# Seven half-block products per chunk pair in the first layer of the second MLP

## The chip, the cores and the metric

The kernel runs on one core of one Trainium2 chip. The metric is the device time of one execution in microseconds (us); less is better. TensorE (PE in the profile) multiplies matrices, VectorE (DVE) and ScalarE (ACT) do elementwise work, GpSimd (POOL) issues a few DMAs here, and SyncE (SP) issues nearly all of them.

## The reference

Attention (a pooled and a banded local softmax attention, added) makes `x` of 2304 tokens x 512. Two MLPs follow, one after the other, each with d_model 512 and d_ff 2048 and its own weights (the host passes them as float64 words):

```python
x = _moe_ref(x)    # h = x @ w_in;  g = h * cos(h);        x = g @ w_out
return _moe2_ref(x)  # h = x @ w_in;  g = maximum(h, 0)**2;  return g @ w_out
```

## The kernel before

Everything is kept transposed: the model or hidden dimension lies on the 128 partitions, the tokens along the free dimension. An fp32 value is split into a high and a low float32r part (`split`: ACT copies to the high part, DVE subtracts to get the low one), and one fp32 product is three matmuls: high weight by high data, high by low, low by high (`mm3`, L641 to L644).

The program has two phases, one for each MLP. A phase goes through five rounds of tokens (`ROUNDS`: four of 512, one of 256), and a round through 16 chunks `f` of 128 hidden units. For each chunk, `mlp_h` (L646) makes 4 x 3 matmuls into a `ps` bank, ACT and DVE apply the nonlinearity and split the result to `gh`, `gl`, and `mlp_o` (L715), some chunks later, makes 4 x 3 matmuls into the four `acc` banks, which sum over all 16 chunks. After the last chunk each `acc` is copied to an `e` tile (two buffers) and stored, to `x2d` in DRAM after phase 0, to the output after phase 1. The first MLP's phase is interleaved with attention units (`unit_g`, `unit_l`); attention for batches 1 to 3 loads pooled sums through accumulating DMAs on the POOL queue.

Weights: `convert` (L253) loads 512 KB of float64 words into a `raw` tile, makes float32 of them with three integer operations on DVE (L265, L272, L277) and splits them. The first-layer weights of the phase stay in 16 `w1` tiles; phase 1's replace phase 0's chunk by chunk during the last round of phase 0 (L838). The second-layer weights are converted in the first round of a phase, saved to `w2d`, and loaded again (`w2`, 512 KB a chunk, three buffers) in every later round.

The order of the program on every engine is written out by `Plan` (L48): each operation has an engine, an assumed cost, a due time (`key`) and what it reads and writes; a list scheduler puts on each engine, in simulated time, what can start first, among equals the one due first. A table `OFF` of offsets shifts due times by operation name and stage. What comes out is a fixed order for each engine; on the chip every instruction waits for its own semaphores, and those queued behind it on its engine wait with it.

Of the kernel before, what the change touches and what calls it, by code (L numbers as in the profile page):

```python
# [40 lines left out]
ORDER = [[0, 1, 2, 3, 4], [0, 2, 3, 4, 1]]  # L41
# [6 lines left out]
class Plan:  # L48
    """The order of the program: operations are put on their engines when what they need is there."""
# [3 lines left out]
    IN_TURN = ("rawi", "rawo", "w2", "p", "pt", "q", "v", "t")  # L53
# [30 lines left out]
    def slow(used, warm, t, cost):  # L84
        """The tensor engine runs at half its clock in a window that follows a mostly idle one."""
# [13 lines left out]
    def order(self):  # L99
# [23 lines left out]
        def room(inst):  # L123
            tag = inst[0]
            held = got[tag]
            if tag in self.IN_TURN and turn[tag][len(held)] != inst:
                return None
            if len(held) < self.bufs[tag]:
                return 0.0
            last = [end[i] for i in self.users[held[-self.bufs[tag]]]]  # L130
            return None if None in last else max(last) + 0.1

        while len(out) < n:
            best = None
            for e, c in cand.items():
                t_min, pick = None, []
                for i in c:
                    t = max(free[e], ready_at[i])
                    for inst in ops[i][5]:
                        x = room(inst)  # L140
# [16 lines left out]
            for inst in new:  # L157
                got[inst[0]].append(inst)
            begin[i] = t
# [42 lines left out]
def body(ctx: ExitStack, tc: tile.TileContext, qb, kw, vw, qp, kp, vp, wi, wo, masks, ident, out_t):  # L202
# [4 lines left out]
        "mx": 4, "sm": 4, "gh": 3, "gl": 3, "e": 2, "acc": 1, "ps": 4,  # L207
    }

    const = ctx.enter_context(tc.tile_pool(name="const", bufs=1))  # L210
    pool = ctx.enter_context(tc.tile_pool(name="work", bufs=2))
    psum = ctx.enter_context(tc.tile_pool(name="psum", bufs=1, space=PSUM))

# [3 lines left out]
    kz = [const.tile([128, 2, 2, PR, KT], F32, name=f"kz{i}") for i in range(2)]  # L217
    pz = [const.tile([128, PR, 2, 2, QT], F32, name=f"pz{i}") for i in range(2)]
# [3 lines left out]
    w1 = [const.tile([128, 2, KD, 128], F32R, name=f"w1_{f}") for f in range(NF)]  # L222
    xh = const.tile([128, KD, 512], F32R, name="xh")
    xl = const.tile([128, KD, 512], F32R, name="xl")
    xr = const.tile([128, KD, XR], F32, name="xr")
    qn_sb = const.tile([128, PR, SD], F32, name="qn_sb")
    qd_sb = const.tile([128, PR, 3, 2, 48], F32, name="qd_sb")
    kd_sb = const.tile([128, PR, SD], F32, name="kd_sb")
    vd_sb = const.tile([SD // 2, 2, DM], F32, name="vd_sb")
    up_sb = const.tile([128, PR, S], F32, name="up_sb")  # L230
    x2d = nc.dram_tensor("x2_dram", [128, KD, NT], F32, kind="Internal").ap()
    w2d = [nc.dram_tensor(f"w2_dram_{p}", [NF, 128, 2, DM], F32, kind="Internal").ap() for p in range(2)]
# [5 lines left out]
    def new(inst, shape, dtype=F32, space=None):  # L238
        p = psum if space else pool
# [14 lines left out]
    def convert(key, lead, name, src, hi, lo, wh, wl):  # L254
        raw, m, a = ("raw" + name[0],) + name[1:], ("wm", name), ("wa", name)

        def load():
            new(raw, [128, 512, 2], I32)
            if wh[1]:
# [21 lines left out]
        op("SP", 1.46, key - lead, load, w=[raw] + wh[0], new=[raw] + wh[1])  # L281
# [3 lines left out]
        split(key + 0.03, 512, hi, lo, lambda: T[a].bitcast(F32), [a], (wh[0], []), wl)  # L285

    def conv_wi(key, lead, ph, f):
        convert(
            key, lead, ("i", ph, f), wi[ph, f],
            lambda: w1[f][:, 0].rearrange("p k n -> p (k n)"), lambda: w1[f][:, 1].rearrange("p k n -> p (k n)"),  # L290
            ([("w1h", f)], []), ([("w1l", f)], []),
        )

    def get_w2(key, ph, r, f):
        w2 = ("w2", ph, r, f)
        if r == ORDER[ph][0]:
# [334 lines left out]

    def load_x2(r, key):
        t0, n = ROUNDS[r]
        for o, c, m in ring(t0, n):
            op(
                "SP", m / 175, key, lambda o=o, c=c, m=m: nc.sync.dma_start(
                    out=xr[:, :, c:c + m], in_=x2d[:, :, t0 + o:t0 + o + m]),
                r=[("x2d", r, c2) for c2 in range(KD)], w=xtok(t0 + o, m),
            )
# [6 lines left out]
    def mlp_h(ph, r, f, key):  # L646
# [3 lines left out]
        for k in range(KD):  # L650
            def f_h(k=k):
                if k == 0:
                    new(hp, [128, 512], space=PSUM)
                mm3(
                    T[hp][:, 0:n], w1[f][:, 0, k], w1[f][:, 1, k], xh[:, k, 0:n], xl[:, k, 0:n], k == 0, k == KD - 1
# [3 lines left out]
                "PE", 3 * (n / 2400 + 0.0025), key + 0.01 * k, f_h,  # L659
                r=[("w1h", f), ("w1l", f), ("xh", k), ("xl", k)], w=[hp], new=[hp] if k == 0 else [],  # L660
# [6 lines left out]
        if ph == 0:  # L667
            def f_k():
                new(ki, [128, 512], I32)
                nc.scalar.activation(out=tt(ki), in_=tt(hp), func=AF.Copy, scale=1.0 / TWO_PI)  # L670

            def f_r():
                new(t, [128, 512])
                nc.vector.scalar_tensor_tensor(  # L674
                    out=tt(t), in0=tt(ki), scalar=-TWO_PI, in1=tt(hp), op0=OP.mult, op1=OP.add
                )

            def f_sin():
                nc.scalar.activation(out=tt(t), in_=tt(t), func=AF.Sin, scale=-1.0, bias=halfpi[:, 0:1])  # L679

            def f_g():
                nc.vector.tensor_tensor(out=tt(t), in0=tt(t), in1=tt(hp), op=OP.mult)  # L682
# [240 lines left out]
```

## Time and profile before

| | us |
|---|---|
| median of 3 runs | 955.86 |
| the 3 runs | 956.81, 955.05, 955.86 |
| span of the profiled execution | 956.2 |
| PE / DVE / ACT busy in the span | 927.4 / 519.2 / 471.7 |

The span runs from the first to the last instruction of one profiled execution; no other time of that execution is shown, so its own time is taken as its span, which lies 0.3 us above the median. Matmuls are pipelined, so that the profile gives each a duration longer than the distance to the next; a rate is read from the distance between starts.

### The profile page before, as it was taken

The numbers are of one execution on the slowest core, as the hardware profiler recorded it, in microseconds if no ns is written. First come the engines' busy times: TensorE is split into PE (matmuls) and PEld (weight loads), VectorE is DVE, ScalarE is ACT, GpSimd is POOL, SyncE is SP. The second block draws the span as 40 slices with busy tenths as digits, with TensorE's granted clock in tenths as the row PEclk, the third lists the DMA queues.
The fourth block names the chain that finished last, engine by engine and source line by source line (L and its number), as shares of the span: only waits on it lengthen the run. The fifth ranks groups of instructions, "written<-read, shape, count | busy, mean of one in ns | idle before, by whom it ended". The sixth has DMA issues, their size and how long they took to land.

```text
span 956.2 us, 13754 instructions
## 1 busy us (share of the span) xinstructions
PE 927.4 (97%) x5312; PEld 765.8 (80%) x5312; DVE 519.2 (54%) x953; ACT 471.7 (49%) x962; POOL 36.8 (4%) x53
## 2 busy tenths in 40 slices
PE   7889999989999999999999999999999999999997
PEld 7677787889877778787888888888888888888897
DVE  7878999645744457344787786662223223222322
ACT  3757787757747767455655533341223223222322
POOL 3030000300210000000000000000000000000000
PEclk9999999989999999999999999999999999999999
DMA  9996665975972242322765675554235233423364
GB/s 283 290 271 173 220 215 207 261 220 175 263 178 89 78 146 96 121 97 90 268 214 177 220 245 196 176 202 140 89 109 165 88 96 107 150 90 109 115 216 133
DMA packets 59857, 162.06 MB, mean 169 GB/s; under 512 B 6544, under 2 KB 16528, under 8 KB 59792
## 3 DMA queue, kind: packets, MB, share of 16 engines
q1 hardware_dynamic: 55184, 149.38, 47.2%
q0 software_dynamic: 4608, 11.80, 6.3%
q8 instruction: 42, 0.69, 0.3%
q14 instruction: 23, 0.19, 0.1%
HBM read 134.94 MB, written 26.21 MB: 169 GB/s over the span
## 4 chain that ended last, share of the span: by engine, by line
PE 85%; DMA 10%; DVE 2%; ACT 1%; SPq 1%; issue 0%; POOL 0%; ACTq 0%; DVEq 0%; POOLq 0%
PE acc L642 14%; PE acc L643 13%; PE acc L644 13%; PE ps L642 13%; PE ps L643 13%; PE ps L644 13%; DMA kd_sb<-in_kp_dram 2%; DMA rawi<-in_wi_dram 2%; PE ps L583 2%; PE ps L546 2%; DMA w<-w_dram 1%; DMA mask_f<-in_masks_dram 1%; PE ps L471 1%; DMA v<-in_vw_dram 1%; DMA qn_sb<-in_qp_dram 1%; PE ps L505 1%
## 5 line engine op out<-in xcount | busy, mean ns | idle before, releaser
L642 PE MATMUL acc<-gh,w 128*128 128x512 f32 (+1 forms) x640 | 240.6, 376 | 4.8 <-DMA w<-w_dram 3.7
L642 PE MATMUL ps<-xh,w 128*128 128x512 f32 (+1 forms) x640 | 241.3, 377 | 2.0 <-DVE t L682 2.0
L644 PE MATMUL ps<-xh,w 128*128 128x512 f32 (+1 forms) x640 | 238.6, 373 | 0.0
L643 PE MATMUL ps<-xl,w 128*128 128x512 f32 (+1 forms) x640 | 238.4, 373 | 0.0
L643 PE MATMUL acc<-gl,w 128*128 128x512 f32 (+1 forms) x640 | 238.1, 372 | 0.0
L644 PE MATMUL acc<-gh,w 128*128 128x512 f32 (+1 forms) x640 | 237.4, 371 | 0.0
L693 ACT ACTIVATE t<-ps 128x512 f32<-128x512 f32 (+1 forms) x80 | 44.5, 556 | 235.8 <-PE ps L644 235.8
L696 DVE SCALAR_TENSOR_TENSOR t<-ps,t 128x512 f32<-128x512 f32 (+1 forms) x80 | 50.9, 638 | 200.5 <-ACT t L693 200.5
L642 PEld LDWEIGHTS acc<-gh,w 128*128 128x128 f32 x640 | 120.9, 189 | 29.6 <-issue 4.8
L642 PEld LDWEIGHTS ps<-xh,w 128*128 128x128 f32 x640 | 120.8, 189 | 26.6 <-DVE t L682 2.9
L643 PEld LDWEIGHTS acc<-gl,w 128*128 128x128 f32 x640 | 121.1, 189 | 22.5 <-DVE gl L248 0.2
L644 PEld LDWEIGHTS acc<-gh,w 128*128 128x128 f32 x640 | 120.8, 189 | 22.3
L644 PEld LDWEIGHTS ps<-xh,w 128*128 128x128 f32 x640 | 120.5, 188 | 22.1
L643 PEld LDWEIGHTS ps<-xl,w 128*128 128x128 f32 x640 | 120.6, 188 | 20.7
L248 DVE TENSOR_TENSOR gl<-t,gh 128x512 fp32r<-128x512 f32 (+1 forms) x160 | 101.6, 636 | 64.5 <-ACT gh L245 61.1
L245 ACT ACTIVATE gh<-t 128x512 fp32r<-128x512 f32 (+1 forms) x160 | 93.6, 586 | 77.3 <-DVE t L696 41.9
L682 DVE TENSOR_TENSOR t<-t,ps 128x512 f32<-128x512 f32 (+1 forms) x80 | 50.3, 632 | 53.1 <-ACT t L679 52.7
L670 ACT ACTIVATE ki<-ps 128x512 int32<-128x512 f32 (+1 forms) x80 | 43.7, 549 | 64.6 <-PE ps L644 63.8
L674 DVE SCALAR_TENSOR_TENSOR t<-ki,ps 128x512 f32<-128x512 int32 (+1 forms) x80 | 50.4, 631 | 32.9 <-ACT ki L670 32.0
L687 ACT ACTIVATE t<-t 128x512 f32<-128x512 f32 (+1 forms) x80 | 46.8, 584 | 26.4 <-DVE t L674 25.5
L679 ACT ACTIVATE t<-t,halfpi 128x512 f32<-128x512 f32 (+1 forms) x80 | 54.1, 679 | 1.8
L245 ACT ACTIVATE w<-wa 128x512 fp32r<-128x512 f32 x64 | 39.8, 624 | 10.1 <-DVE wa L277 9.8
(66 smaller groups left out, 755.7 us busy)
## 6 DMA issues: line engine op xcount, KB each, us to landing
w<-w_dram SPq DMA_DIRECT2D x128, 512.0 KB, 3.3
rawo<-in_wo_dram SPq DMA_DIRECT2D x32, 512.0 KB, 4.3
rawi<-in_wi_dram SPq DMA_DIRECT2D x32, 512.0 KB, 4.9
w_dram<-w SPq DMA_DIRECT2D x32, 512.0 KB, 3.0
v<-in_vw_dram SPq DMA_DIRECT2D x20, 256.0 KB, 4.8
kz<-in_kw_dram SPq DMA_DIRECT2D x40, 128.0 KB, 4.9
q<-in_qb_dram SPq DMA_DIRECT2D x20, 232.0 KB, 4.8
vd_sb<-in_vp_dram POOLq DMA_DIRECT2D x16, 288.0 KB, 7.1
```

The source lines that it names most:

```text
L245: nc.scalar.activation(out=hi(), in_=src(), func=AF.Copy)
L248: nc.vector.tensor_tensor(out=lo(), in0=src(), in1=hi().bitcast(F32), op=OP.subtract)
L642: nc.tensor.matmul(ps, w_hi, r_hi, start=first, stop=False)
L643: nc.tensor.matmul(ps, w_hi, r_lo, start=False, stop=False)
L644: nc.tensor.matmul(ps, w_lo, r_hi, start=False, stop=last)
L670: nc.scalar.activation(out=tt(ki), in_=tt(hp), func=AF.Copy, scale=1.0 / TWO_PI)
L674: nc.vector.scalar_tensor_tensor(out=tt(t), in0=tt(ki), scalar=-TWO_PI, in1=tt(hp), op0=OP.mult, op1=OP.add)
L679: nc.scalar.activation(out=tt(t), in_=tt(t), func=AF.Sin, scale=-1.0, bias=halfpi[:, 0:1])
L682: nc.vector.tensor_tensor(out=tt(t), in0=tt(t), in1=tt(hp), op=OP.mult)
L687: "ACT", act(n), key + 0.2, lambda: nc.scalar.activation(out=tt(t), in_=tt(t), func=AF.Abs), w=[t]
L693: nc.scalar.activation(out=tt(t), in_=tt(hp), func=AF.Relu)
L696: nc.vector.scalar_tensor_tensor(out=tt(t), in0=tt(hp), scalar=0.0, in1=tt(t), op0=OP.max, op1=OP.mult)
```

## The change

Phase 1 becomes a form of its own; phase 0 keeps its rounds and its code, while the cost that the plan assumes for one matmul of n columns goes from n/2400 + 0.0025 to n x 0.0004375 + 0.007.

- Phase 1 has three rounds R of 768 tokens, each in two halves of 384, and goes through 8 pairs `p` of chunks. The first layer of a pair (2 chunks, 2 x 256 inner, 2 halves of tokens) is done as seven products in place of eight. Each product takes 6 matmuls of 384 columns (`big_h`) into one of two PSUM banks `pp0`, `pp1`, in turn. ACT copies the first product out; DVE adds the others from PSUM into `ua` and `c` tiles (seven additions of 384 columns).
- The data operands (`operands`, once per round) are seven split tiles made from `xr`: 4 subtractions and 7 splits of 768 columns.
- The weight operands (`conv1`, once per pair, emitted at the third round of phase 0) are made from the raw words, with 4 sums of 256 columns and splits of 2 x 256, 2 x 256, 2 x 256 and 256 columns, and stored to a DRAM tensor `w1d` (seven blocks of 256 KB a pair). `big_h` loads each block for each product again, into the `gh` and `gl` buffers (three each), once the last `gh` and `gl` of phase 0 are written. The conversion of the second MLP's `w_in` in the last round of phase 0 goes.
- The square of the relu, and its split, are done at 768 columns (`big_g`: DVE, ACT, DVE). The parts lie in the memory of `xh`, `xl` and one `w1` tile.
- The second layer (`big_o`) makes, for each chunk and each of 4 output blocks, three matmuls of 512 and three of 256 columns; the 256-column results of two blocks share a bank (`acx0`, `acx1`). After a round there are four `e` tiles for the 512 part and two for the shared banks, through the same two buffers.
- The attention tiles sit in a pool of their own, which is closed and reused for the operands.

```diff
+            for h in range(2):
+                def f_p(h=h, ws=ws, x=x, b=b):
+                    ww = [T[ws][:, i, 128 * h:128 * h + 128] for i in range(2)]
+                    xx = [T[xo(R, x)][:, i, h] for i in range(2)]
+                    mm3(T[f"pp{b}"][:, 0:HALF], ww[0], ww[1], xx[0], xx[1], h == 0, h == 1)
...
+            if nm == "p1":
+                op(
+                    "ACT", act(HALF), k, lambda ps=ps: nc.scalar.activation(out=uv(0), in_=ps(), func=AF.Copy),
+                    r=[pp], w=[u],
+                )
+            elif nm == "p2":
+                add(k, lambda: part(0, 0), lambda: uv(0), [u], [c[0]])
+            elif nm == "p6":
+                add(k, lambda: uv(0), lambda: uv(0), [], [u])
+            elif nm == "p7":
+                add(k, lambda: uv(1), lambda: uv(0), [u], [v])
+            elif nm == "p5":
+                add(k, lambda: part(1, 1), lambda: uv(1), [v], [c[1]])
+                add(k + 0.01, lambda: uv(0), lambda: uv(0), [], [u])
+            elif nm == "p3":
+                add(k, lambda: part(0, 1), lambda: uv(0), [u], [c[0]])
+                big_g(R, p, 0, k + 0.02)
+            else:
+                add(k, lambda: part(1, 0), lambda: uv(1), [v], [c[1]], sub=True)
+                big_g(R, p, 1, k + 0.02)
...
+            op("SP", 0.73, k - 12.0, f_w, r=[("w1d", p, n // 2), ("last",)], w=[ws], new=[ws])
...
+            op("PE", 3 * 0.231, k, f_b, r=g, w=[("accb", c)])
+            op("PE", 3 * 0.119, k + 0.01, f_x, r=g, w=[("acx", c // 2)])
...
+            op("SP", 1.46, k - 12.0, load, r=[("conv",)], w=[raw], new=[raw])
+            op("DVE", dve2(512), k, f1, r=[raw], w=[m], new=[m])
+            op("DVE", dve(512), k + 0.01, f2, r=[raw, m], w=[a], new=[a])
+            op("DVE", dve(512), k + 0.02, f3, r=[raw], w=[a])
...
+            op("ACT", act(256 * n), k, f_hi, r=[t], w=[st], new=[st])
+            op("DVE", dve(256 * n), k + 0.01, f_lo, r=[t], w=[st])
+            op("SP", 0.73 * n, k + 0.5, f_st, r=[st], w=[("w1d", p, j)])
...
+    for R in range(NBIG):
+        if R:
+            operands(R, big_when[R - 1, 1], big_when[R - 1, 2], big_step * 5)
+        for p in range(PAIRS):
+            t_p = big_when[R, p]
+            for i in range(2):
+                get_w2b(t_p + big_step * (0.8 + 0.5 * i), R, 2 * p + i)
+            q = (R, p - 1) if p else (R - 1, PAIRS - 1)
+            for i in range(2):
+                if i:
+                    big_h(R, p, t_p, big_step)
+                if R or p:
+                    big_o(q[0], 2 * q[1] + i, big_when[q] + big_step * (LAG + 0.5 * i), big_step / 2)
```

## Rows read from the trace of the kernel before

**Rows 1.** The page: busy time, share of the span and instructions of each engine.

```profile
PE 927.4 (97%) x5312; PEld 765.8 (80%) x5312; DVE 519.2 (54%) x953; ACT 471.7 (49%) x962; POOL 36.8 (4%) x53
```

**Rows 2.** Stretches: length, busy time of each engine, granted clock, DMA share, GB/s.

```profile
160.00:200.00 40.00, 35.17 (x253) 31.15 (x252) 24.31 (x58) 27.89 (x59) 9.75 (x13) 0.95 1.00 282
240.00:280.00 40.00, 39.02 (x265) 32.02 (x264) 24.05 (x46) 23.52 (x42) 10.18 (x13) 1.00 0.97 239
...
480.00:520.00 40.00, 40.00 (x174) 32.28 (x173) 32.34 (x54) 21.82 (x37) 0.00 (x0) 1.00 0.57 194
...
680.00:720.00 40.00, 40.00 (x174) 32.31 (x173) 11.67 (x17) 10.92 (x19) 0.00 (x0) 1.00 0.29 93
```

**Rows 3.** Timeline of PE in phase 1: 100 starts of 512 columns, 176 of 256.

```profile
699.49 0.40 PE L644 MATMUL ps<-xh,w 128*128 128x512 f32 x1
...
722.72 0.39 PE L642 MATMUL ps<-xh,w 128*128 128x512 f32 x1
...
909.11 0.28 PE L642 MATMUL ps<-xh,w 128*128 128x256 f32 x1
...
930.03 0.28 PE L644 MATMUL acc<-gh,w 128*128 128x256 f32 x1
```

**Rows 4.** Groups by shape on PE, whole span: count, busy, mean ns, idle before.

```profile
L642 PE MATMUL ps<-xh,w 128*128 128x512 f32 x512 | 204.2, 399 | 2.0 <-DVE t L682 2.0
...
L642 PE MATMUL ps<-xh,w 128*128 128x256 f32 x128 | 37.1, 290 | 0.0
```

**Rows 5.** Groups by shape from 640 us on: weight loads of one line.

```profile
L643 PEld LDWEIGHTS acc<-gl,w 128*128 128x128 f32 x260 | 49.0, 188 | 9.0 <-DVE gl L248 0.2
```

**Rows 6.** Groups by shape on DVE, whole span.

```profile
L248 DVE TENSOR_TENSOR gl<-t,gh 128x512 fp32r<-128x512 f32 x128 | 88.1, 689 | 45.4 <-ACT gh L245 42.0 <-PE acc L644 1.4
...
L272 DVE SCALAR_TENSOR_TENSOR wa<-rawo,wm 128x512 int32<-128x512 int32 x32 | 22.0, 688 | 0.7
...
L248 DVE TENSOR_TENSOR gl<-t,gh 128x256 fp32r<-128x256 f32 x32 | 13.5, 422 | 19.1 <-ACT gh L245 19.1
...
L265 DVE TENSOR_SCALAR wm<-rawo 128x512 int32<-128x512 int32 x32 | 13.4, 418 | 3.3 <-DMA rawo<-in_wo_dram 3.3
...
L248 DVE TENSOR_TENSOR xl<-xr,xh 128x384 fp32r<-128x384 f32 x8 | 4.2, 553 | 0.1
```

**Rows 7.** Timeline between the phases: last first-layer matmul, last low part, first of phase 1.

```profile
535.30 0.40 PE L644 MATMUL ps<-xh,w 128*128 128x512 f32 x1
...
540.31 0.68 DVE L248 TENSOR_TENSOR gl<-t,gh 128x512 fp32r<-128x512 f32 x1
...
541.80 0.39 PE L642 MATMUL ps<-xh,w 128*128 128x512 f32 x1
```

**Rows 8.** Timeline of the end of the span.

```profile
948.80 0.38 ACT L744 ACTIVATE e<-acc 128x256 f32<-128x256 f32 x1 [1.05 <-PE acc L644]
...
949.54 0.28 PE L644 MATMUL acc<-gh,w 128*128 128x256 f32 x1
951.05 0.38 ACT L744 ACTIVATE e<-acc 128x256 f32<-128x256 f32 x1 [1.87 <-DMA out_dram<-e]
951.53 0.42 DVE L742 COPY e<-acc 128x256 f32<-128x256 f32 x1 [1.95 <-DMA out_dram<-e]
```

**Rows 9.** DMA issues: count, KB each, median us from issue to landing.

```profile
w<-w_dram SPq DMA_DIRECT2D x128, 512.0 KB, 3.3
...
rawi<-in_wi_dram SPq DMA_DIRECT2D x32, 512.0 KB, 4.9
...
out_dram<-e SPq DMA_DIRECT2D x16, 256.0 KB, 2.3
...
kd_sb<-in_kp_dram POOLq DMA_DIRECT2D x12, 288.0 KB, 6.7
```

**Rows 10.** Waits of PE before 440 us: total, times, longest.

```profile
PE acc L642 <- DMA w<-w_dram: 3.7, 2, 3.4
```

**Rows 11.** Timeline of the SP queue: the last save of first-round weights.

```profile
173.66 0.33 SPq L304 DMA_DIRECT2D w_dram<-w  x1
```

More of the change, by code (lines that the diff above doesn't have):

```diff
@@ L258, in load @@
             new(raw, [128, 512, 2], I32)
+            if first:
+                new(home, [128, 2, 2, KD, 128], F32R)
             if wh[1]:
@@ L279, in f3 @@
             )
-        op("SP", 1.46, key - lead, load, w=[raw] + wh[0], new=[raw] + wh[1])
+        op("SP", 1.46, key - lead, load, w=[raw] + wh[0], new=[raw] + wh[1] + ([home] if first else []))
         op("DVE", dve2(512), key, f1, r=[raw], w=[m], new=[m])
@@ L630, in split_x @@
                 )
[L632 to L639, printed above, removed]
     def mm3(ps, w_hi, w_lo, r_hi, r_lo, first, last):
@@ L701, in mlp_h @@
+        op("ACT", act(n), key, f_k, r=[hp], w=[ki], new=[ki])
+        op("DVE", dve(n), key + 0.1, f_r, r=[ki, hp], w=[t], new=[t])
+        op(
+            "ACT", act(n), key + 0.2, lambda: nc.scalar.activation(out=tt(t), in_=tt(t), func=AF.Abs), w=[t]
+        )
+        op("ACT", act(n, 0.09), key + 0.3, f_sin, r=[("halfpi",)], w=[t], table="sin")
         op("DVE", dve(n), key + 0.4, f_g, r=[hp], w=[t])
@@ L713, in mlp_h @@
         split(key + 0.5, n, g_hi, g_lo, lambda: tt(t), [t], ([gh], [gh]), ([gl], [gl]))
+        plan.writer[("last",)] = plan.writer[gh] + plan.writer[gl]
     def mlp_o(ph, r, f, key):
@@ new lines, in late_banks, with gtok, gpart @@
+    def late_banks():
+        if "pp0" not in T:
+            for i, nm in enumerate(("pp0", "pp1", "acx0", "acx1")):
+                T[nm] = psum.tile([128, 512], F32, tag="ps", name=nm, bufs=4)
+            for i in range(2):
+                T["ua", i] = pool.tile([128, 512], F32, tag="ki", name=f"ua{i}", bufs=2)
+    def gtok(R, f):
+        i = (R * NF + f) % 3
+        return ("w1", "g") if i == 2 else ("bg", i)
+    def gpart(part, R, f):
+        i = (R * NF + f) % 3
+        if i == 2:
+            return T["w1", "g"][:, BIG * part:BIG * part + BIG]
+        return (xh, xl)[part].rearrange("p k n -> p (k n)")[:, BIG * i:BIG * i + BIG]
@@ new lines, in big_g, with f_g, f_gh, f_gl @@
+    def big_g(R, p, i, key):
+        t, f = ("c", i), 2 * p + i
+        def f_g():
+            nc.vector.scalar_tensor_tensor(out=T[t], in0=T[t], scalar=0.0, in1=T[t], op0=OP.max, op1=OP.mult)
+        g = gtok(R, f)
+        home = [g] if R == 0 and f == 2 else []
+        def f_gh():
+            if home:
+                new(g, [128, 4 * KD * 128], F32R)
+            nc.scalar.activation(out=gpart(0, R, f), in_=T[t], func=AF.Copy)
+        def f_gl():
+            nc.vector.tensor_tensor(out=gpart(1, R, f), in0=T[t], in1=gpart(0, R, f).bitcast(F32), op=OP.subtract)
+        op("DVE", dve(BIG), key, f_g, w=[t])
+        first = [("xh", x) for x in range(KD)] + [("xl", x) for x in range(KD)] if R == 0 and f < 2 else []
+        op("ACT", act(BIG), key + 0.01, f_gh, r=[t], w=[g] + first, new=home)
+        op("DVE", dve(BIG), key + 0.02, f_gl, r=[t], w=[g])
@@ new lines, in body @@
+    for n, r in enumerate(ORDER):
+        first, last = n == 0, n == NR - 1
+        t_r = when[0, r, 0]
+        t_e = when[0, r, NF - 1]
+        if first:
+            for f in range(NF):
+                conv_wi(when[0, 0, f] - 10.0, 12.0, f)
+        if n == 2:
+            step_c = (when[0, ORDER[4], 10] - t_r) / PAIRS
+            for p in range(PAIRS):
+                conv1(t_r + step_c * p, step_c, p)
+        split_x(0, r, t_r - 0.5)
+        if not last:
+            e = need(r + 1)
+            emit_units(units[done:e], t_r, t_e - 8.0)
+            done = e
+        else:
+            operands(0, t_r + 10.0, t_r + 25.0, 30.0)
+        for f in range(NF):
+            t_f = when[0, r, f]
+            get_w2(t_f, 0, r, f)
+            mlp_h(0, r, f, t_f)
+            for x in late:
+                if x[3] <= t_f + 2.0 * step[r]:
+                    mlp_o(*x)
+            late = [x for x in late if x[3] > t_f + 2.0 * step[r]]
+            late.append((0, r, f, t_f + 1.6 * step[r]))
@@ L847, in body @@
+    for i in range(2):
+        big_o(NBIG - 1, NF - 2 + i, big_when[NBIG - 1, PAIRS - 1] + big_step * (LAG + 0.5 * i), big_step / 2)
     with tc.manual_schedule():
```

402 lines of the change are left out of this document (307 added, 95 removed).

## The prediction, made before the changed kernel was run

> **What bounds the kernel now.** I read the page's busy times first, then stretches of 40 us, then the timeline of PE, and last the end of the span and the DMA rows. PE is busy for 97% of the span, no other engine for more than 54% [rows 1]. That share hides two kinds of stretch. In phase 1 PE is busy for 40.00 of 40.00 us at a granted clock of 1.00 (the 2.4 GHz level), even where DVE has 32.34 us of work [rows 2]. In phase 0 it falls to 35.17 and 39.02 us just where the DMA share is 1.00 and 0.97 [rows 2]; there the longest wait of PE for the second-layer weights lies [rows 10]. So phase 1 is worth what PE issues, and phase 0 what its order and DMA leave to PE.
>
> The rate of issue comes from distances between starts. 100 steps of 512 columns take 722.72 - 699.49 = 23.23 us, 0.2323 us each; 176 steps of 256 columns take 930.03 - 909.11 = 20.92 us, 0.1189 us each [rows 3]. The kernel has six lines of each shape with 512 and 128 instructions a line [rows 4]; half are phase 1's: 1536 x 0.2323 + 384 x 0.1189 = 402.5 us. From the first matmul of phase 1 at 541.80 to the end of the last, 949.54 + 0.12, lie 407.9 us [rows 7, 8]; the other 5.4 us are 23 second-layer matmuls of phase 0 that come after 541.80. Nothing is left over: phase 1 has no idle PE time to win.
>
> **Matmuls of phase 1.** 384 columns do not occur in the trace as a matmul. Half-way between the two spacings is 0.1756 us. The bounds are proportions: 3/4 of 0.2323 is 0.1742, 3/2 of 0.1189 is 0.1784. I take 0.1756, since both ends of the line are measured. First layer after: 24 pairs x 42 = 1008 x 0.1756 = 177.0 us (175.6 to 179.8). Second layer: 576 x (0.2323 + 0.1189) = 202.3 us; it loses 1 us, since more of its columns come as 256. Together 379.3, that is 15.8 us a pair, against 402.5: **-23.2 us** (-24.6 to -20.4).
>
> The weight loads beside these matmuls show 188 ns each and overlap them [rows 5]: at 256 columns a new matmul still starts every 118.9 ns, less than one load's duration, so at 384 columns they have more room. The Trainium skill says in "TensorE: Matmul & The Clock Gate" (section "The mechanism") that a weight load overlaps running matmuls only when it targets another row group, and puts a load of 128 columns at 128/1.2 = 107 ns (section "LDWEIGHTS"). By that, every full-height matmul here would pay 107 ns more than its columns, the change's larger number of matmuls would cost more than its columns save (an estimate from that page: 573.6 us before, 576.5 after, +2.9). The spacings of [rows 3] lie below what that would give at both widths, so I don't sum by it; the mechanism stays as rival E.
>
> **Eviction and DVE in phase 1.** The adds have 384 columns, 0.553 us; wide operations go from 0.422 at 256 and 0.689 at 512 to 0.956 us at 768, by the same slope [rows 6]. A pair has 7 x 0.553 + 4 x 0.956 = 7.7 us on DVE. Round 0 adds the conversion of two second-layer chunks, 2 x (0.418 + 2 x 0.688 + 0.689) = 5.0, and the operands of the next round, 11 x 0.956 / 8 = 1.3: 14.0 of 15.8 us, 88%. The densest comparable stretch of before has 81% and PE full [rows 2]. Rounds 1 and 2 have 57% and 49%. ACT has three operations a pair and two more in round 0; I cost it at nothing, hidden beside DVE. A product's bank is needed again two products later. With the second layer spread between (8.4 us over 7 products) that is 1.05 + 1.2 us after it ended, and its add takes 0.553, or 1.1 for the product with two adds: covered, unless a 0.956 us operation or a conversion sits ahead of it on DVE. The first pair has no second-layer work between: 7.7 us of DVE against 7.4 of PE. I take 1 us for that and 0.25 us for each pair of round 0: **+3 us**. From below 0; from above 10% of round 0, 12.6 us, if DVE in fixed order loses 15%.
>
> **Streamed weights.** A pair loads 7 x 256 KB and 2 x 512 KB: 2.88 MB in 15.8 us, 182 GB/s. In round 0 two more saves of 512 KB and the next round's data make 4.13 MB, 261 GB/s. The light stretch of phase 1 moves 93 GB/s at a share of 0.29, 320 at a full one; the full stretches of phase 0 moved 282 and 239 [rows 2]. A 256 KB transfer lands 2.3 us after its issue, one of 512 KB after 3.3 [rows 9], and six blocks can be under way, which is 6/7 of a pair, 13.5 us. Hidden in rounds 1 and 2; in round 0 hidden if the full rate is nearer to 320 than to 239, since these are whole rows of 2 KB and 4 KB. Uncovered it is rival A.
>
> **The border of the phases.** The first products wait for a load that itself waits for the last low part of phase 0, done at 540.31 + 0.68 = 541.0; plus 2.3 to 3.3 us, 543.3 to 544.3 [rows 7, 9]. Behind the waiting load on SP sit the other blocks. PE, however, has 50 second-layer matmuls to go after 535.30 (27 up to 541.80, 23 after), 11.6 us, until 547.1: hidden with 3 us to spare. If the order leaves only the last chunk there (2.8 us), it costs 5.8. I take **+0.5**.
>
> **The end.** Now four copies go through two `e` buffers; the second use of a buffer starts 951.05 - 948.80 = 2.25 us after the first, 1.87 of it for the store to leave, and the last copy ends 4.2 us before the span does [rows 8]. After it there are six tiles of 512 columns, so three uses of each buffer, each 0.6 + 2.3 = 2.9 us [rows 9]. With the first copy 0.2 us after its four-block group's first result, 3.15 us ahead of the last matmul, the other buffer 1.05 us later, the last copy ends 0.2 + 1.05 + 2 x 2.9 + 0.65 = 7.7 us and the span about 4.65 us later: 9.2 us behind the last matmul, against 6.5 now. **+2.7** (0 to +4). Between rounds the same copies are covered by products.
>
> **Phase 0.** Its code stays; its order does not. The plan's cost of a 512 matmul goes from 0.2158 to 0.231, near the measured 0.2323, so due times move and the offset table meets another plan. On DVE the sums and splits of `conv1` take 8 x (2 x (0.418 + 2 x 0.688) + 5 x 0.422 + 3 x 0.689) = 62 us in place of 16 x 2.48 = 40 us, spread over three rounds where DVE is busy 24 of 40 us, not put in the last one: covered. The DMA side is not. Each pair loads 1.05 MB and stores 1.83. The scheduler starts what can start, and SP is mostly idle, so the raw loads go out soon after the last conversion, whose save is issued at 173.66 [rows 11], and not at their due time: into the two full stretches. The first two raw loads, 1.05 MB at 282 GB/s, put 3.7 us in front of a wait that already reaches PE [rows 2, 10]. A whole pair, 2.88 MB, is 10.2 us; one in each stretch 20.4. From below, the idle PE time of these stretches, 4.8 + 1.0 us, could go: -5.8. I take **+4**, the nearest row being that wait.
>
> On the POOL queue an accumulating load of 288 KB takes 6.7 us [rows 9], and four of them follow one another for each array. The Trainium skill ("DMA: Bandwidth & Descriptors", section "Queues, rings and completion order") says that each DMA engine goes round-robin among the queues with work. By that, more SP traffic leaves the POOL queue its turn, and only SP's own loads behind `conv1` are late, so the second stretch would add nothing to the 4. No row separates the two queues, so both bounds stay.
>
> **Sum.** -23.2 + 3 + 0.5 + 2.7 + 4 = -13.0: 956.2 to 943.2 us of span, and with the 0.3 us between span and median **943 us**.
>
> **Rivals.**
> A. Round 0 becomes bound by DMA. At 239 GB/s a pair's 4.13 MB take 17.3 us, 1.5 more than PE, 11.8 in the round in place of the 3: 952 us. For: the two full stretches. Against: the 320 of large rows.
> B. Phase 0 pays a whole pair of `conv1` traffic in one full stretch, 10.2 for 4: 949. For: DMA shares of 1.00 and 0.97. Against: little in those stretches waits for one transfer.
> C. Slower: products wait for their banks throughout. Place: the adds on DVE, between 768-wide operations and in a chain through one `ua` tile. Without the 3 the gain is 16.0 us; over 168 products it is gone at 0.095 us each. At 0.15 us it is 25 us of waits, 965. For: two banks instead of four `ps`, fixed order. Against: 1.2 us of other PE work behind each product, DVE at half in two of three rounds.
> D. Better: phase 0 stays as it is and nothing waits: -23.2 + 2.7, 935.
> E. The change doesn't do what it says: at 384 columns the spacing is a weight load's 0.188 us [rows 5], 1008 x 0.0124 = 12.5 more: 955. Against: the 0.1189 at 256.
>
> **Chances.** Forecast 0.44, with a range of its own of 937 to 948; D 0.17, B 0.14, C 0.11, A 0.10, E 0.04. Less than 0.2% is what a measurement of this kernel can't tell from no change: 953.9 to 957.8. Faster: 0.44 + 0.17 and most of B (0.11), A (0.07), E (0.01) = 0.80; within: 0.02 each of A, B, E = 0.06; slower: C and the tails, 0.14. The range 932 to 955 leaves out C, D's lower part (phase 0 gaining its 5.8) and the upper tail of B.
>
> **What would show it.** Starts of 384-column matmuls every 0.1756 us (E: 0.188). PE idle in phase 1 under 4 us, all in round 0 (A: waits for the streamed block; C: waits of products for DVE in every round). First product straight behind the last second-layer matmul of phase 0. 9 us from the last matmul to the end. The first product about 4.5 us later than phase 1 would start now, 547; if it comes more than 10 us later, phase 0 was the step I mis-sized, and if it comes earlier, the order there became better. The prediction is wrong as a whole if phase 1's matmuls span more than 392 us.

## The result, and the profile after

The changed kernel takes **969.06 us** (median of 4 runs, 967.38 to 971.97) against 956.23 for the kernel before on the same chip: ratio 1.0115, 95% interval 1.0075 to 1.0155. It is slower by 1.2%, clear of noise, since the interval leaves out 1; forecast was 943. Its profiled execution took 968.87 us with a span of 967.1; in every experiment, too, a run's own time lies 1.7 to 1.9 us above its span, so the "0.3 us between span and median" that the forecast carried was not that distance: with 1.8 the forecast would have been 945. By the same 1.8 the profiled execution of the kernel before, with a span of 956.2, took about 958.0, more than its median; so the spans differ by 10.9 us where the medians differ by 12.8.

The page of the changed kernel, busy times:

```profile
PE 912.2 (94%) x5552; PEld 794.4 (82%) x5552; DVE 622.0 (64%) x1106; ACT 449.4 (46%) x889; POOL 36.8 (4%) x53
```

PE is busy for 15 us less than in [rows 1] and the span is 11 us longer: PE idles 26 us more. Stretches of the changed kernel (columns as in [rows 2]):

```profile
160.00:200.00 40.00, 32.65 (x236) 28.07 (x230) 29.54 (x69) 23.21 (x47) 10.13 (x13) 0.91 0.97 274
200.00:240.00 40.00, 32.13 (x261) 30.59 (x261) 23.80 (x54) 26.01 (x68) 0.00 (x0) 0.91 0.83 290
240.00:280.00 40.00, 32.40 (x291) 27.91 (x290) 32.66 (x74) 28.87 (x65) 2.42 (x5) 0.88 0.86 283
280.00:320.00 40.00, 39.07 (x197) 31.56 (x197) 29.45 (x57) 24.87 (x47) 7.35 (x9) 0.99 0.97 286
...
680.00:720.00 40.00, 39.86 (x227) 36.72 (x225) 31.49 (x48) 13.92 (x20) 0.00 (x0) 1.00 0.77 249
```

The same view of the kernel before, the two stretches that [rows 2] leaves out:

```profile
200.00:240.00 40.00, 40.00 (x369) 37.33 (x368) 21.76 (x52) 29.09 (x82) 0.00 (x0) 0.97 0.55 174
...
280.00:320.00 40.00, 38.98 (x207) 31.23 (x206) 19.00 (x35) 29.81 (x63) 0.00 (x0) 1.00 0.29 91
```

Before, the DMA had a pause between its two full stretches (share 0.55) and another behind them (0.29). Now it has none from 160 to 320 us. PE idles 7.35 + 7.87 + 7.60 + 0.93 = 23.75 us in these 160, against 6.83 before, and the granted clock, a mean between its two levels, is lower in all four.

When the rounds of phase 0 end is read from SP's first store of a round's `x` to DRAM, second to fifth round. Before, then after:

```profile
242.72 0.91 SPq L748 DMA_DIRECT2D x_dram<-e  x2
...
357.23 0.80 SPq L748 DMA_DIRECT2D x_dram<-e  x2
...
463.70 1.41 SPq L748 DMA_DIRECT2D x_dram<-e  x2
...
549.56 3.02 SPq L748 DMA_DIRECT2D x_dram<-e  x2
```

```profile
265.52 0.40 SPq L752 DMA_DIRECT2D x_dram<-e  x1
...
387.16 1.11 SPq L752 DMA_DIRECT2D x_dram<-e  x2
...
492.92 0.80 SPq L752 DMA_DIRECT2D x_dram<-e  x2
...
572.03 1.04 SPq L752 DMA_DIRECT2D x_dram<-e  x2
```

The second round ends 22.8 us late, the third 29.9, the fourth 29.2, the fifth 22.5 (before, first-layer matmuls of phase 1 were already mixed into its end). The first ends 2.4 us late, at 178.98 against 176.57. So nearly all of the loss lies in the second and third rounds of phase 0, whose code the change leaves as it was.

PE at the border (last second-layer matmuls of phase 0, first products), and later the one wait for a streamed block:

```profile
572.28 0.39 PE L660 MATMUL acc<-gh,w 128*128 128x512 f32 x1
572.51 0.33 PE L658 MATMUL pp<-xo_b,gh 128*128 128x384 f32 x1
...
573.58 0.33 PE L658 MATMUL pp<-xo_b,gh 128*128 128x384 f32 x1
...
574.44 0.33 PE L660 MATMUL pp<-xo_b,gl 128*128 128x384 f32 x1
...
580.23 0.41 PE L658 MATMUL pp<-xo_t,gh 128*128 128x384 f32 x1 [2.65 <-DMA gh<-w_dram]
...
581.45 0.53 PE L658 MATMUL pp<-xo_b,gl 128*128 128x384 f32 x1
...
584.33 0.49 PE L658 MATMUL pp<-xo_t,gh 128*128 128x384 f32 x1
```

Here a 384-column matmul starts every (574.44 - 573.58) / 5 = 0.172 us; over all of phase 1 the mean step, without those at waits and at the lower clock, is 0.176. After the wait of 2.65 us PE first goes on at the full rate; then, from 581.45 on, nine steps take 584.33 - 581.45 = 2.88 us, 0.32 each: the lower clock level.

The end, last matmul and last copies:

```profile
959.15 0.28 PE L1086 MATMUL acx<-w,w 128*128 128x256 f32 x1
...
961.86 0.60 ACT L1098 ACTIVATE e<-acc 128x512 f32<-128x512 f32 x1 [1.51 <-DMA out_dram<-e]
962.58 0.69 DVE L1110 COPY e<-acx 128x512 f32<-128x512 f32 x1 [3.07 <-ACT e L1098]
```

What PE waited for between 160 and 300 us (total, times, longest):

```profile
PE acc L658 <- ACT e L749: 6.2, 1, 6.2
PE acc L658 <- DMA w<-w_dram: 5.9, 3, 4.4
PE ps L658 <- DVE t L697: 5.4, 2, 3.4
```

What ACT waited for there, what SP waited for, and timelines of SP, ACT and PE, all of the changed kernel:

```profile
ACT rawo L822 <- DMA w_dram<-rawo: 15.6, 4, 7.4
```

```profile
SPq L830 <- DVE rawo L825: 19.4, 6, 7.0
```

```profile
168.33 0.93 SPq L771 DMA_DIRECT2D rawi<-in_wi_dram  x2
...
182.21 0.62 SPq L752 DMA_DIRECT2D x_dram<-e  x1
...
191.64 0.60 ACT L749 ACTIVATE e<-acc 128x512 f32<-128x512 f32 x1 [4.28 <-DMA x_dram<-e]
...
192.29 0.58 PE L658 MATMUL acc<-gh,w 128*128 128x256 f32 x1 [6.24 <-ACT e L749]
```

Three different waits make up 17.5 of the 23.75 us of idle time. One is `w`, late on PE. One goes over ACT: the copy of `acc` at 191.64 waits 4.28 us for the last but one store of `x` to leave its `e` buffer, issued at 182.21, 9.4 us earlier (the four stores of this round land 5.7 to 14.8 us after their issue, 11.2 in the median; before, 3.9 to 13.5 and 9.5), and PE waits 6.24 us for the `acc` bank; before it was 1.1. The third is DVE. The new conversion's raw loads begin at 168.33; ACT's 15.6 us are its splits, which wait for their buffer's last store, with whatever stands behind them in ACT's order. SP's 19.4 us are stores of the conversion, which wait for DVE to finish the split; loads of `w` and stores of `x` stand behind them in SP's order.

### The profile page after: what moved, and what is told of

Same layout as the page of the kernel before. It is cut to its first block, busy times and chain, and to the rows that moved or that the text cites. A ratio compares the mean times of both kernels' runs of the same rounds, so it can differ in the third digit from the quotient of the medians.

```text
span 967.1 us, 14804 instructions
## 1 busy us (share of the span) xinstructions
PE 912.2 (94%) x5552; PEld 794.4 (82%) x5552; DVE 622.0 (64%) x1106; ACT 449.4 (46%) x889; POOL 36.8 (4%) x53
## 4 chain that ended last, share of the span: by engine, by line
PE 70%; DMA 16%; DVE 6%; ACT 5%; issue 1%; SPq 1%; POOL 0%; ACTq 0%; DVEq 0%; POOLq 0%
PE acc L658 9%; PE acc L659 9%; PE acc L660 9%; PE pp L660 6%; PE pp L659 6%; PE pp L658 6%; PE ps L658 5%; PE ps L659 4%; PE ps L660 4%; DMA rawi<-in_wi_dram 4%; DMA kd_sb<-in_kp_dram 2%; PE acx L1084 2%; PE acx L1086 2%; PE acx L1085 2%; DMA out_dram<-e 2%; DMA w<-w_dram 1%
## 5 line engine op out<-in xcount | busy, mean ns | idle before, releaser
L658 PE MATMUL acc<-gh,w 128*128 128x512 f32 (+1 forms) x320 | 121.9, 381 | 12.2 <-ACT e L749 6.2
L658 PE MATMUL ps<-xh,w 128*128 128x512 f32 (+1 forms) x320 | 125.4, 392 | 7.5 <-DVE t L697 7.5
L659 PE MATMUL ps<-xl,w 128*128 128x512 f32 (+1 forms) x320 | 120.3, 376 | 0.0
L660 PE MATMUL ps<-xh,w 128*128 128x512 f32 (+1 forms) x320 | 120.0, 375 | 0.0
L659 PE MATMUL acc<-gl,w 128*128 128x512 f32 (+1 forms) x320 | 119.0, 372 | 0.9 <-DVE gl L267 0.9
L660 PE MATMUL acc<-gh,w 128*128 128x512 f32 (+1 forms) x320 | 118.8, 371 | 0.0
L1016 DVE TENSOR_TENSOR c<-ua,pp 128x384 f32<-128x384 f32 x96 | 53.0, 552 | 54.9 <-PE pp L660 54.6
L658 PEld LDWEIGHTS acc<-gh,w 128*128 128x128 f32 x320 | 61.2, 191 | 24.8 <-ACT e L749 6.6
L658 PEld LDWEIGHTS ps<-xh,w 128*128 128x128 f32 x320 | 62.4, 195 | 20.4 <-DVE t L697 8.3
L660 PEld LDWEIGHTS ps<-xh,w 128*128 128x128 f32 x320 | 62.3, 195 | 10.5
L659 PEld LDWEIGHTS acc<-gl,w 128*128 128x128 f32 x320 | 61.3, 192 | 11.0 <-DVE gl L267 1.3
L660 PEld LDWEIGHTS acc<-gh,w 128*128 128x128 f32 x320 | 61.2, 191 | 10.7 <-DVE w L267 0.4
L659 PEld LDWEIGHTS ps<-xl,w 128*128 128x128 f32 x320 | 62.6, 196 | 8.9
L267 DVE TENSOR_TENSOR gl<-t,gh 128x512 fp32r<-128x512 f32 (+1 forms) x80 | 50.5, 633 | 17.8 <-ACT gh L264 17.4
```

What stands on the lines that cost most here:

```text
L267: nc.vector.tensor_tensor(out=lo(), in0=src(), in1=hi().bitcast(F32), op=OP.subtract)
L658: nc.tensor.matmul(ps, w_hi, r_hi, start=first, stop=False)
L659: nc.tensor.matmul(ps, w_hi, r_lo, start=False, stop=False)
L660: nc.tensor.matmul(ps, w_lo, r_hi, start=False, stop=last)
L1016: nc.vector.tensor_tensor(out=out(), in0=a(), in1=ps(), op=OP.subtract if sub else OP.add)
```

## The experiments

The change touches phase 0 in two ways: the conversion `conv1` runs from the end of its first round into the third (raw loads from 168 us, though due in the third), and the assumed matmul cost alters the order. In the expectations T1 is the first theory (T1a its transfers, T1b its DVE and ACT work), T2 the second (T2a through due times, T2b through the durations that the plan simulates); O means the order, L the load; "the change" is the kernel after.

**The two-by-two.** First, the conversion later: emitted at the fourth round, its loads from 384 us on (with the old cost, below, from 352).

```diff
-        if n == 2:
+        if n == 3:
+            plan.writer[("conv",)] = plan.writer[("gh", 0, 2, NF - 1)]
```

> The changed kernel, with the weight-sum conversion held back: its raw loads come only after the last split of the third round of phase 0 (about 380 us instead of 168 us). T1 (the early conversion in the two full DMA stretches costs phase 0 its 25 us): the second round takes 66 to 70 us from store to store in place of 86, the third about 115, the first product starts at 547 to 555 us, time 944 to 950. T2 (the plan's new matmul cost and the offsets tuned for the old one spoil the order): nothing moves, time 964 to 972. Half of each: 955 to 960.

Measured 976.36 us, ratio 1.0194 (1.0161 to 1.0227). Slower than the change, and above T2's range too: T1 alone doesn't explain it.

Second, the kernel before with only the new assumed cost, in its three places.

```diff
-                "PE", 3 * (n / 2400 + 0.0025), key + 0.01 * k, f_h,
+                "PE", 3 * (n * 0.0004375 + 0.007), key + 0.01 * k, f_h,
...
-    step = [24 * (n / 2400 + 0.0025) for _, n in ROUNDS]
+    step = [24 * (n * 0.0004375 + 0.007) for _, n in ROUNDS]
```

> The kernel before, with only the plan's assumed matmul cost changed to the new formula, in both phases. T1: the order hardly suffers, 953 to 960. T2: phase 0 is 15 to 25 us longer, 970 to 980.

Measured 988.65, ratio 1.0330 (1.0294 to 1.0365). No work is added, and 32 us are lost: T2 holds, by more than its range. (ACT loads its function tables 40 times in the new order, 34 in the old, 1.28 us each; what those six cost was not tested.)

Third, the change with the old assumed cost (the same lines back).

> The changed kernel with the old matmul cost formula in phase 0; the conversion starts as early as before. T1: 964 to 972, first product near 572 us. T2: 944 to 950, first product near 550 us.

Measured 967.63, ratio 1.0112 (1.0072 to 1.0152): no better than the change. Fourth, both edits at once.

> Both edits: conversion held back until 380 us, old cost formula. T1: equal to the held-back kernel within 4 us (944 to 950). T2: equal to the one with old costs. If each costs half, this one alone reaches 944 to 948, the other two 955 to 960.

Measured **943.37**, ratio 0.9854 (0.9814 to 0.9895). With both causes out, the time is the forecast's 943; that it fits so well is in part luck, as is shown under "Why the prediction was wrong". Either cause alone brings the loss back: + 24.3 for the early conversion, + 33.0 for the new cost; both together, + 25.7. They don't add.

**The new assumed cost.** Only its due times, then only its durations, in the kernel before:

```diff
-    step = [24 * (n / 2400 + 0.0025) for _, n in ROUNDS]
+    step = [24 * (n * 0.0004375 + 0.007) for _, n in ROUNDS]
```

> The kernel before with the new formula only in the due times of the chunks (step), the operations' own assumed costs as before. T2a (the due times, against which the offsets were fitted, are what moved the order): 975 to 990, like the whole formula. T2b (the simulated durations are): 953 to 962.

```diff
-                "PE", 3 * (n / 2400 + 0.0025), key + 0.01 * k, f_h,
+                "PE", 3 * (n * 0.0004375 + 0.007), key + 0.01 * k, f_h,
...
-                "PE", 3 * (n / 2400 + 0.0025), key + 0.01 * c, f_o,
+                "PE", 3 * (n * 0.0004375 + 0.007), key + 0.01 * c, f_o,
```

> The counterpart: new formula in the simulated durations of the matmuls, old due times. T2a: 953 to 962. T2b: 975 to 990. If any change of the plan's numbers spoils a fitted order: both 970 and more.

Measured 967.84 (ratio 1.0116, 1.0078 to 1.0154) and 981.53 (1.0260, 1.0221 to 1.0300). Either half costs, the durations more; 967.84 lies between the ranges of T2a and T2b, so neither theory is right alone. To see whether the cost itself or the offset table is to blame, the table was emptied, with the old cost and with the new one:

```diff
-OFF = {('PE|unit_g.f_s|ps|wps', 1): 42.1, ('ACT|softmax.f_norm|wp', 1): 8.0,
...
+OFF = {}
```

> The kernel before with its offset table emptied and its own assumed matmul cost. It is the base for the next run. Theory T3 (the table is fitted to this cost, so it carries what the order is worth): 975 to 995 us, about where the kernel before stands with the new cost, 989. Rival T4 (the new cost itself gives a worse order, the table little): 955 to 965.

> The kernel before with an empty offset table and the new assumed matmul cost. T3: within 8 us of the run with the empty table and the old cost, either side, since nothing is left for the new cost to upset. T4: 20 to 30 us above that run.

Measured 1003.73 (ratio 1.0496, 1.0474 to 1.0517) and 1005.24 (1.0508, 1.0489 to 1.0527). Without the table the two costs are 1.5 us apart, and their intervals overlap. The table is worth 48 us with the cost it came with and 17 with the other: T3. (The level, expected 975 to 995, was missed.)

One place where the new cost hurts can be seen. In the kernel before with the new cost, the timelines of DVE and of PE, and the stretch:

```profile
293.60 0.92 DVE L461 COPY qd_sb<-qn_sb 64x576 f32<-64x576 f32 x2 [11.48 <-DMA qn_sb<-in_qp_dram]
```

```profile
295.30 1.81 PE L583 MATMUL ps<-pz,v 128*64 128x116 f32 x16 [11.16 <-DVE t L682]
```

```profile
280.00:320.00 40.00, 28.84 (x144) 23.04 (x143) 14.38 (x23) 15.97 (x27) 4.39 (x5) 0.87 0.50 109
```

A copy for the attention stands in DVE's fixed order and waits 11.48 us for an accumulating load; behind it stands `t` of the MLP, and PE waits 11.16 us for that. The wait on DVE alone doesn't cost this: the kernel before has one of 8.6 us at the same copy, but there PE waits only 0.8 us for the `t` behind it. The remedy is to put the copy on another engine, whose order has room:

```diff
-                    nc.vector.tensor_copy(
+                    nc.gpsimd.tensor_copy(
```

> The kernel before with the new assumed cost, and that copy issued on GpSimd in place of DVE; the plan's order is the same. If DVE standing 11.5 us behind the copy's wait is what makes PE wait 11 us there: 972 to 978 us, 11 to 16 less than the 989 without the move. If PE would have been late for other work anyway: 985 to 989.

Measured 975.19, ratio 1.0198 (1.0180 to 1.0215): 13 us of the 32 are gone, as expected. The copy now waits on POOL, and PE is full in that stretch:

```profile
296.05 1.37 POOL L461 COPY qd_sb<-qn_sb 64x576 f32<-64x576 f32 x2 [6.88 <-DMA qn_sb<-in_qp_dram]
```

```profile
280.00:320.00 40.00, 40.00 (x204) 32.32 (x203) 18.81 (x30) 25.73 (x47) 5.43 (x7) 1.00 0.57 139
```

The other 19 us have no single place that I could show: from 200 to 240 us PE is busy for 33.73 us there, 40.00 in the kernel before, with 4.4 us of waits for `w` and 3.8 for `gh`.

**The early conversion.** Into the kernel with late conversion and old cost (943.37) went the early transfers alone, then the early DVE and ACT work alone, as operations of the plan:

```diff
+PACE = ((0, 15), (1, 4), (1, 10), (2, 0), (2, 3), (2, 7), (2, 10), (2, 12))
...
+            op("SP", 1.46, key, load, r=[("go", p)], w=[raw], new=[raw])
+        for j in range(4):
+            raw, m = raws[j % 2], 1024 if j < 3 else 512
+            op(
+                "SP", 1.46 * m / 1024, key + 2.0 + 2.0 * j, lambda j=j, raw=raw, m=m: nc.sync.dma_start(
...
+            if (r, f) in PACE:
+                extra(t_f, PACE.index((r, f)), plan.writer[("gh", 0, r, f)])
```

> The changed kernel with conversion held back and old costs (943 us), plus transfers alone: eight times, at the times where the early conversion ran (about 170 to 350 us), two loads of 512 KB and stores of 3 x 512 and 256 KB to a scratch tensor that nobody reads. T1a (the early conversion hurts by its transfers): 958 to 968, rounds two and three of phase 0 longer by 20 us in all. T1b (it hurts by its work on DVE and ACT): 942 to 948.

```diff
+            op("DVE", dve2(512), key, f1, r=[raw, ("go", p)], w=[m], new=[m])
+            op("DVE", dve(512), key + 0.01, f2, r=[raw, m], w=[a], new=[a])
+            op("DVE", dve(512), key + 0.02, f3, r=[raw], w=[a])
...
+            op("ACT", act(n), k, f_hi, r=[t], w=[st], new=[st])
+            op("DVE", dve(n), k + 0.01, f_lo, r=[t], w=[st])
```

> The same base, plus the early conversion's DVE and ACT work alone, eight times at the same places, on raw words that are loaded once; its results are not used and nothing is stored. T1a: 943 to 949. T1b: 958 to 968. Both in part: each near 952 to 956.

Measured 976.75 (ratio 1.0209, 1.0156 to 1.0262) and 966.62 (1.0106, 1.0065 to 1.0147): + 33 and + 23, together far more than the 24 they were to explain. The experiment is confounded: what is planned also reorders the rest. The waits of DVE and PE show it; transfers alone, then work alone:

```profile
DVE qd_sb L487 <- DMA qn_sb<-in_qp_dram: 19.8, 1, 19.8
...
PE acc L660 <- DVE gl L268: 16.3, 1, 16.3
```

```profile
DVE qd_sb L487 <- DMA qn_sb<-in_qp_dram: 10.0, 1, 10.0
...
PE ps L609 <- DVE t L698: 9.0, 1, 9.0
```

The copy blocks PE again in both. In the base DVE waits 9.9 us for the same load, but PE no more than 2.4 us for DVE: another order stands behind the copy. So order and load were taken apart: first the early conversion in the plan, beside the real, late one, with operations that issue nothing.

```diff
+            op("SP", 1.46, k - 12.0, nothing, r=[("conv",)], w=[raws[n]], new=[raws[n]])
+            op("DVE", dve2(512), k, nothing, r=[raws[n]], w=[m], new=[m])
...
+            op("ACT", act(256 * n), k, nothing, r=[t], w=[st], new=[st])
+            op("DVE", dve(256 * n), k + 0.01, nothing, r=[t], w=[st])
+            op("SP", 0.73 * n, k + 0.5, nothing, r=[st], w=[("scr", p, j)])
```

> The same base (943 us); the early conversion stands in the plan, in its loads, DVE and ACT operations and stores, but issues nothing: the chip runs the order that leaves room for it, without its load. Theory O (the disturbed order costs the time, not the load): 955 to 968. Theory L (the load itself does): 941 to 948.

Then the plan untouched, and the transfers issued next to loads of `w` that are there anyway (2 loads of 512 KB, 3.5 stores of 512 KB for each of eight pairs):

```diff
+HOOKS = ((1, 1), (1, 3), (1, 6), (1, 8), (1, 11), (1, 13), (2, 0), (2, 2), (2, 3), (2, 5), (2, 7), (2, 8), (2, 10), (2, 11), (2, 12), (2, 14))
...
+                if (r, f) in HOOKS:
+                    hidden(*divmod(HOOKS.index((r, f)), 2))
```

> The same base and exactly its order; the plan does not know of the same 8 x (2 + 3.5) transfers of 512 KB that are issued beside second-layer weight loads of rounds two and three of phase 0. O: 943 to 948. L by transfers: 955 to 972.

And DVE and ACT work alone, behind operations that are there anyway:

```diff
+        for n in wide:
+            nc.vector.tensor_tensor(out=x[:, 0:n], in0=x[:, 0:n], in1=x[:, 0:n], op=OP.subtract)
...
+            nc.scalar.activation(out=T["xa"].bitcast(F32), in_=T["xd"].bitcast(F32), func=AF.Copy)
...
+            more_dve(r, (512, 256) if r == 2 else (512,))
...
+            more_dve(r, (512, 512) if r == 2 else (256,))
```

> The same base and order; DVE gets about 1.1 us more work a chunk in round two and 2.5 in round three, ACT 0.6, which the plan does not know of and nobody uses. O: 943 to 948. L by work on DVE: 952 to 966.

Measured 947.35 (ratio 0.9896, 0.9861 to 0.9932), 956.04 (0.9996, 0.9974 to 1.0017) and 950.85 (0.9940, 0.9913 to 0.9967). These ran on another chip, beside another set of runs of the kernel before, than the base did, so ratios are compared, with the base's 0.9854 (0.9814 to 0.9895) and 956.5 us: order + 4.0 us, transfers + 13.6, DVE and ACT work + 8.2, in sum 25.8 for the 24.7 that separate the base from the change with the old cost (1.0112). The transfers and the work are resolved; the order's 4 us are not, since the intervals overlap. So O fails for the early conversion: its order costs little, where 955 to 968 were expected. For the transfers L holds; the work's 950.85 lies between both ranges. (The order run spreads the due times of the operations that issue nothing over the third round alone; in the change they reach into the fifth.) The first product of phase 1 says the same in the profiled executions: 544.79 us in the base, 550.14 with the order, 555.86 with the transfers, 552.01 with the work, 568.90 with the real early conversion; 5.4 + 11.1 + 7.2 = 23.7 of 24.1 us.

Where the transfers act, in the order that the base has. First the base: the longest waits of DVE for a load and of PE before 440 us, and issues in 160 to 300 us (count, KB, median us to landing):

```profile
DVE qd_sb L486 <- DMA qn_sb<-in_qp_dram: 9.9, 1, 9.9
...
PE acc L658 <- DMA w<-w_dram: 4.2, 2, 2.1
```

```profile
w<-w_dram SPq DMA_DIRECT2D x25, 512.0 KB, 4.7
kd_sb<-in_kp_dram POOLq DMA_DIRECT2D x8, 288.0 KB, 7.1
```

The same with the transfers, and ahead of it two stretches:

```profile
200.00:240.00 40.00, 37.62 (x338) 35.60 (x338) 19.00 (x46) 28.25 (x82) 0.00 (x0) 0.99 0.92 338
240.00:280.00 40.00, 36.19 (x280) 29.77 (x279) 27.49 (x53) 25.63 (x46) 9.31 (x12) 1.00 1.04 300
```

```profile
DVE qd_sb L503 <- DMA qn_sb<-in_qp_dram: 11.2, 1, 11.2
...
PE acc L675 <- DMA w<-w_dram: 7.9, 3, 4.8
```

```profile
w<-w_dram SPq DMA_DIRECT2D x23, 512.0 KB, 6.7
kd_sb<-in_kp_dram POOLq DMA_DIRECT2D x8, 288.0 KB, 8.1
```

The pause in the DMA between the full stretches is filled. PE is busy 2.4 and 3.7 us less in these two stretches than in the base (40.00 and 39.89), `w` lands 2.0 us later, and PE waits 7.9 us for it, against 4.2. Of the accumulating loads on the POOL queue `kd_sb` lands 1.0 us later and `qn_sb` 1.2 (8.9 against 7.7), `vd_sb` no later (7.3). SP is held up as well: the added stores wait for their own loads six times, 10.0 us in all, and what stands behind them in SP's order leaves late (the second pair of `x` stores of the first round at 196.79 us, in the base at 183.46). How much of the 13.6 us comes from the bytes on full queues, and how much from SP's fixed order, no run separates. With the DVE work instead, PE waits for DVE (`t`) five times for 5.6 us, in the base twice for 4.6; PE's idle time from 160 to 400 us grows from 10.1 to 15.0 us, and no single wait carries that.

**A better kernel.** The base, with the copies of the shared second-layer banks going through `t` buffers, which are idle then, in place of `e`:

```diff
-                y = ("e", "x", c, R)
+                y = ("t", "x", c, R)
```

> The changed kernel with conversion held back and old costs, and the copies of the two shared banks in the two free `t` buffers of phase 0 instead of the two `e` buffers. The waits of second-layer matmuls for those copies (3.0 us, and the lower clock behind them) go, and the last copies come 2 us earlier: 937 to 941. If the waits only move elsewhere: 942 to 945.

Measured 937.20, ratio 0.9797 (0.9764 to 0.9829): in the expected range, but not told apart from the base, as the intervals overlap. With the copy on GpSimd as well (the edit above):

> Old assumed cost, late conversion, shared-bank copies in t buffers, and one copy of a pooled-attention operand, which waits for an accumulating load, issued on GpSimd in place of DVE. If DVE standing behind that wait costs time in this order too: 932 to 935 us. If what stands behind it is not late: 937, give or take 2.

Measured **934.27**, ratio 0.9763 (0.9738 to 0.9788): the fastest here, 2.4% under the kernel before, and 3.5% under the change by the quotient of the two ratios. Both edits together are resolved against the base; from the one without the GpSimd copy it is not told apart, as the intervals overlap: in that order DVE stood 10.5 us behind the copy, but PE's longest wait for `t` was 3.0.

## Why the prediction was wrong

The spans differ by 967.1 - 956.2 = + 10.9 us, forecast - 13.0. Piece by piece:

| | forecast | measured |
|---|---|---|
| Phase 0 and border | + 4 + 0.5 | + 26.0 |
| Phase 1's matmuls, eviction and waits | - 23.2 + 3 | - 16.4 |
| The end | + 2.7 | + 1.3 |
| Sum | - 13.0 | + 10.9 |

Phase 0: 572.51 plus the three second-layer matmuls behind it (0.7) against 541.80 + 5.4 before. Phase 1: from 572.51 to 959.27, less these 0.7, is 386.1 against 402.5. The end: 967.1 - 959.27 = 7.8 against 6.5.

**The step that failed is "Phase 0": "I take +4, the nearest row being that wait", between -5.8 and 20.4.** All of the 23.9 us between forecast and result, but 2.4, lies there, and even the upper bound was too low. Its parts:

- *"The DMA side is not [covered]"*: right in place, wrong in size. The raw loads go out at 168.33 us, in the first round, for a conversion due from the third on, as worked out. But 4 us were for one pair's two loads in front of one wait. The transfers measure + 13.6 us: eight pairs load every stretch, the pause from 200 to 240 us as well, and their stores hold up SP. I had bounded the cost by the two full stretches and not looked at the ones between and behind them, nor at SP's order.
- *"spread over three rounds where DVE is busy 24 of 40 us ... covered"*: wrong. DVE and ACT work in the same rounds costs + 8.2 us with the order unchanged, of 57.5 us of added work on DVE (64 operations of 0.687 us, 32 of 0.423). A busy share of 60% doesn't cover all of it when each `t` and `gl` has to be ready in its turn: [rows 6] show DVE waiting 42.0 us for ACT in one line, a chain through both engines. That an operation put into this chain delays its end is my reading; the waits of PE for `t`, 5.6 us against 4.6, don't show it.
- *"due times move and the offset table meets another plan"*: seen, and bounded on the wrong side. I gave the new plan no loss of its own, only a gain of up to 5.8 us from idle PE time that could go. In the kernel before it costs + 32. The table is fitted to its cost: a better constant in a plan of fitted offsets is a perturbation like any other.
- These costs are not independent. Beside the early conversion the new assumed cost adds 1.4 us, which is within the noise, not 33. In the change DVE's copy waits 4.3 us for its load, 11.48 in the kernel before with the new cost: what DVE has to convert stands ahead of the copy then. With the new cost and the conversion held back the copy waits 10.1 us again, and PE 9.8 us for `t`. That fits, but that this is why they don't add was not tested.

**What was right.** Phase 1: 384 columns every 0.176 us in the mean (forecast 0.1756); PE busy for 382.8 of 386.8 us; no wait of a product for its bank (rival C), and one wait of 2.65 us for a streamed block in all (rival A). Of the 386.1 us 379.3 were forecast for matmuls alone, and the steps at the full rate add up to 379.7. The other 6.4 are that wait (2.8 us with its step), the lower clock behind it (1.6), two waits for `e` at the ends of rounds (1.6), which the prediction had as covered by products, and four slower steps (0.4). None of it is a product that waits for DVE, which the + 3 stood for. In 680 to 720 us the DMA moves 249 GB/s at a share of 0.77 and PE is busy for 39.86. The border: the first product starts 0.23 us after the last matmul before it. Rival E's spacing, the 0.188 of a weight load, is not the mean here, 0.176. The Trainium skill ("TensorE: Matmul & The Clock Gate", section "The mechanism") says in one line that a weight load overlaps running matmuls only when its row group differs; by that line full-height loads would not overlap, and the trace is against it here as at the other widths. The same section also lets a load into the background weight buffer be pulled ahead, and with that the spacings are not at odds. The end cost 1.4 us less than forecast.

**What was luck.** The base of the experiments, with phase 0 put back, takes 943.37 us, the forecast to the digit. Its first product and last matmul:

```profile
544.79 0.33 PE L658 MATMUL pp<-xo_b,gh 128*128 128x384 f32 x1
...
936.66 0.28 PE L1086 MATMUL acx<-w,w 128*128 128x256 f32 x1
```

Read like the table above, its profiled execution (span 945.0, time 946.8, the slowest of its four) has phase 0 at - 1.7 us where + 4.5 was forecast, phase 1 at - 11.2 where - 20.2 was forecast (5.7 us of it waits for `e` and streamed blocks), and the end at + 1.7. Phase 0 without the early conversion came out better than forecast and phase 1 worse; the sum agrees because the two cancel.

Rival B (949) named the place of the loss and 10.2 us for its DMA part, which measures 13.6. The argument against it, "little in those stretches waits for one transfer", is what the 7.9 us of waits for `w`, against 4.2, speak against. On the queues: the Trainium skill ("DMA: Bandwidth & Descriptors", section "Queues, rings and completion order") lets each DMA engine take turns among the queues with work. By that, surplus traffic on SP's queue would delay SP's own loads most. The trace agrees in direction: `w` goes from 4.7 to 6.7 us, `kd_sb` from 7.1 to 8.1, `vd_sb` stays at 7.3. It doesn't follow, as I had put it, that only SP's loads are late.

## What to carry to other kernels

Where an order is written out by a planner with fitted offsets, run an edit of the planner's constants alone before anything is built on it: it can cost more than the change it comes with, and the code of the stretch that pays does not change at all. A pause in a resource between two full stretches is not spare; price what fills it as you would in the full ones. An operation that waits for a long load belongs on an engine on which nothing stands behind it.

## What the hardware showed that was not expected

- Short waits cost more than they last. After PE waited 2.65 us, nine steps ran at 0.32 us in place of 0.176; in the second round of phase 0 a wait of 4.42 us ahead of 206.85 us was followed by 256-column steps of 0.21 us in place of 0.12:

```profile
206.85 0.55 PE L658 MATMUL acc<-gh,w 128*128 128x256 f32 x1 [4.42 <-DMA w<-w_dram]
207.20 0.41 PE L659 MATMUL acc<-gl,w 128*128 128x256 f32 x1
207.42 0.41 PE L660 MATMUL acc<-gh,w 128*128 128x256 f32 x1
```

  The granted clocks of the four stretches from 160 to 320 us fall short of 1.00 by 0.31 in sum, before by 0.08. As a mean over time that is 0.23 x 40 = 9 us of PE's work at most, since the clock is also low while PE idles. What it took can be estimated from busy times: up to the first product PE idles 43.25 us, before 22.45 up to 541.80, so 20.8 of phase 0's 26.0 us are idle time; the other 5.2 are PE being busy longer with the same work.

- In the rows shown here with DMA shares of 0.92 to 1.04 the rate was anywhere between 239 and 338 GB/s: the share alone doesn't say how much the queues move.
